# Top-k attention with a PReLU feed-forward: pairs prepared earlier, the last batch in another order, statistics from halves of fp32

## The chip, the cores and the metric

The kernel runs on one core of one Trainium2 chip. The metric is the device time of one execution in microseconds (us). Three runs of the kernel before gave 913.7 to 915.7, with a median of 914.88.

## What is computed

```python
def _attn_ref(q, k, v):                 # 8 batches, 8 heads, 576 tokens, 64 dims
    scores = (1 / sqrt(64)) * q @ k.T
    kth = np.partition(scores, -32)[..., -32]        # 32nd largest of each row
    scores = np.where(scores >= kth, scores, -1e9)
    attn = softmax(scores)
    return attn @ v

def reference(...):
    x = attn_out as (4608 tokens, 512)
    h = x @ w_in                        # 512 x 2048
    g = max(h, 0) + alpha * min(h, 0)
    return g @ w_out                    # 2048 x 512
```

## The kernel before, in words

**Tiles, pairs, batches.** The unit of the attention is a tile: 128 query rows against 576 keys. Two heads form a pair, whose queries and keys lie transposed in one buffer (`qkT`, one head in each half of the partitions). A pair has nine tiles (TPP = 9): tiles j = 0 to 7 are the four 128-row chunks of its two heads (chunk j // 2, head j % 2), and tile 8 holds the last 64 rows of both heads. There are 32 pairs (NPAIR), so NT = 288 tiles; four pairs form a batch of 576 tokens. P0 = 28 is the first pair of the last batch, N0 = 252 its first tile.

**What a tile needs.** TensorE computes the scores (L314). ScalarE shifts them by a guessed threshold of the row (L323), counts with a Sign pass how many lie above it (L329) and takes the exponential (L334). VectorE flips signs so that the wanted element is among the 24 largest (L345), finds them (L355, L370, L372), picks the limit and makes the mask (L419). GpSimd multiplies mask and exponential (L429); the last six tiles are multiplied on VectorE (L426). A DMA transposes the weights (L442), TensorE multiplies them with v (L488), and the result is divided by its row sum: `av_rz` on VectorE and `av_out` on ScalarE (L517).

**Preparing a pair.** The threshold comes from each row's mean and spread, which `prep_plan` (L166) works out for a pair in seventeen steps: q and k are transposed on TensorE (L175, L188, L196) and copied to `qkT` by ScalarE (L178, L192, L200); q is copied a second time, as bf16, to `qTb` (L180, L201); the 128 x 130 Gram matrix of k is built from fp32 operands (L206); `pe_r`, `dve_p` and `pe_s` (L212 to L241) turn it into the sums, for which `qTb` is read; eight small VectorE steps make the threshold. The transposes and the Gram matrix share one PSUM buffer (tag `pa`), and `pr`, `st` and the products with v (`pu`) share two (tag `pd`).

**The feed-forward.** Once a block of tokens is normalised and transposed (`x_turn`, L544), `mlp_steps` (L626) yields its steps: `ph` steps for the first product, each with a ScalarE activation (L644), and for each 128 tokens three `pz` steps with one copy to the output tile (L661). A block of 128 tokens has four `ph` and three `pz` steps.

**The order is written by hand.** The whole program is laid out tick by tick, one tile per tick (L758 to L842). In tick n the tile n + 1's scores are issued, flip works on tile n - 1, the search on tiles n - 2 and n - 3, and mask and weights on tile n - 7. `put(tick, engine, f)` places other work; a pair's steps stand at fixed distances before `BASE[p]` (L284), and its loads 18 ticks before it (L760). Feed-forward steps wait in the queue `back` and are taken from its front against a credit of 1.9 a tick at a cost of 0.9 or 1.5 (L787 to L799): one a tick, or two where `nb` is 2. Each engine executes its instructions strictly in this order.

**The last batch.** Its first two pairs run nine tiles each; the last two (PA, PB) alternate by chunk (L154). For these, `av_last`, `rz_last` and `out_last` (L521 to L542) handle one chunk of both pairs at a time, and each chunk is then a feed-forward block of 128 tokens.

Of the kernel before, what the change touches and what calls it, by code (L numbers as in the profile page):

```python
# [30 lines left out]
def kernel(  # L31
# [10 lines left out]
    nc = tc.nc  # L42
    B, H, S_, D = q.shape
# [5 lines left out]
    NPAIR = (B * H) // 2  # L49
    KPB = H // 2  # L50
    TPP = 9
    NT = NPAIR * TPP
# [4 lines left out]
    V1 = D + 1  # L57
    HC = S // 2
    P0 = NPAIR - KPB
    N0 = P0 * TPP  # L60
# [29 lines left out]
    prep = main.enter_context(tc.tile_pool(name="prep", bufs=2))  # L90
# [5 lines left out]
    ps_d = main.enter_context(tc.tile_pool(name="ps_d", bufs=2, space=PS))  # L96
# [30 lines left out]
    pairs = {}  # L127
# [21 lines left out]
                          vf[hA + 1, 64:S, :].rearrange("(c p) d -> p c d", p=128))  # L149

    ORDER = [divmod(n, TPP) for n in range(N0)]
    ORDER += [(p, j) for p in (P0, P0 + 1) for j in range(TPP)]
    PA, PB = P0 + 2, P0 + 3
    ORDER += [(p, j) for js in ((0, 1), (8,), (2, 3), (4, 5), (6, 7)) for p in (PA, PB) for j in js]  # L154
    units, unit_of = [], {}
    n = 0
    while n < NT:
        m = 1 if ORDER[n][1] == 8 and ORDER[n + 1][1] != 8 else 2
# [1 line left out]
            unit_of[n + i] = (n, m, i)  # L160
        units.append((n, m))
        n += m
    BASE = {p: TPP * p for p in range(P0)}
    BASE.update({P0: N0, P0 + 1: N0 + 8, PA: N0 + 14, PB: N0 + 20})

    def prep_plan(p):  # L166
        d = pairs[p]
        GK = GKs[p % 2]
        ns = slice(p * TPP, p * TPP + TPP)

        def pe_q():
            d["qkT"] = qkTs[p % NQ]
            d["pq"] = ps_a.tile([128, 512], FP32, name="pq", tag="pa")
            for c in range(4):
                nc.tensor.transpose(d["pq"][:, c * 128:(c + 1) * 128], d["q"][:, c, :], ident_f)  # L175

        def act_q():
            nc.scalar.copy(d["qkT"][:, 0, 0:512], d["pq"])  # L178
            d["qTb"] = prep.tile([128, S], BF16, name="qTb", bufs=2)
            nc.scalar.copy(d["qTb"][:, 0:512], d["pq"])  # L180

        def act_v():
            nc.scalar.copy(d["v"][:, :, 0:D], d["st_v"])
# [14 lines left out]

        def act_t():
            nc.scalar.copy(d["qkT"][:, :, 512:S], d["pt"])  # L200
            nc.scalar.copy(d["qTb"][:, 512:S], d["pt"][:, 0, :])  # L201

        def pe_g():
            d["pg"] = ps_a.tile([128, 130], FP32, name="pg", tag="pa")
            for c in range(5):
                nc.tensor.matmul(d["pg"], d["k"][:, c, 1:129], d["k"][:, c, :],  # L206
                                 start=(c == 0), stop=(c == 4))

        def act_g():
# [2 lines left out]
        def pe_r():  # L212
            d["P"] = prep.tile([128, S], BF16, name="P", bufs=1)
            d["pr"] = []
            for n0, n1 in ((0, 512), (512, S)):
                pr = ps_d.tile([128, n1 - n0], FP32, name="pr", tag="pd")
                for r in (slice(0, 64), slice(64, 128)):
                    nc.tensor.matmul(pr[r], GK[r, 1 + r.start:65 + r.start], d["qTb"][r, n0:n1],
                                     start=True, stop=True)
                d["pr"].append((n0, n1, pr))  # L220

        def dve_p():
            d["km"] = prep.tile([128, 2], BF16, name="km", bufs=2)
            nc.vector.tensor_tensor(d["km"], GK[:, 0:1].to_broadcast([128, 2]), bones, ALU.mult)
            for n0, n1, pr in d["pr"]:
                nc.vector.tensor_tensor(d["P"][:, n0:n1], pr, d["qTb"][:, n0:n1], ALU.mult)  # L226

        def pe_s():
            st = ps_d.tile([128, 2, TPP], FP32, name="st", tag="pd")
# [55 lines left out]
        dvx = "dve" if p < 2 else "dvx"  # L285
# [195 lines left out]
    def x_tiles(b):  # L481
        if b not in xb:
            xb[b] = prep.tile([128, 4, DM], BF16, name="xb", bufs=1)
            xm[b] = prep.tile([64, DM], BF16, name="xm", bufs=1)

    def av_one(o_, d, wT, side, cs):
        for c in range(5):
            nc.tensor.matmul(o_, wT[:, 4 * side + c, cs], d["v"][:, 5 * side + c, :],  # L488
                             start=(c == 0), stop=(c == 4))
# [12 lines left out]
    def av_rz(p, g):  # L502
        d = pairs[p]
        d["rz", g] = rz = attn.tile([128, 6], FP32, name="rz", bufs=4)
        nc.vector.reciprocal(rz[:, 0:4], d["pu", g][:, 0:4, D])
        if g == 1:
            nc.vector.reciprocal(rz[0:64, 4:6], d["pu", g][0:64, 4:6, D])
# [10 lines left out]

    pul = {}

    def av_last(i):  # L521
        m = 128 if i < 4 else 64
        pul[i] = pu = ps_d.tile([128, 4, V1], FP32, name="pu", tag="pd")
        for s, p in enumerate((PA, PB)):
            d = pairs[p]
            for side in range(2):
                cs = slice(0, 128) if i < 4 else slice(64 * side, 64 * side + 64)
                av_one(pu[0:m, 2 * s + side, :], d, d["wT", i] if i < 4 else d["wTm"], side, cs)

    def rz_last(i):  # L530
        m = 128 if i < 4 else 64
        rz = attn.tile([128, 6], FP32, name="rz", bufs=4)
        nc.vector.reciprocal(rz[0:m, 0:4], pul[i][0:m, :, D])
        pul[i] = pul[i], rz

    def out_last(i):
        m = 128 if i < 4 else 64
        pu, rz = pul.pop(i)
        dst = xb[B - 1][:, i, :] if i < 4 else xm[B - 1]
        nc.vector.tensor_tensor(  # L540
            dst[:, 256:512].rearrange("p (s d) -> p s d", s=4), pu[0:m, :, 0:D],
            rz[0:m, 0:4].unsqueeze(2).to_broadcast([m, 4, D]), ALU.mult)  # L542

    def x_turn(b, chunks):  # L544
        for i in chunks:
            c0 = (b * S + 128 * i) % NX
            if b == B - 1:
                c0 = b * S % NX + (64 + 128 * i if i < 4 else 0)
            if i < 4:
                nc.sync.dma_start_transpose(xT[:, :, c0:c0 + 128], xb[b][:, i, :])  # L550
            else:
                nc.sync.dma_start_transpose(xT[:, :, c0:c0 + 64], xm[b])
# [63 lines left out]
    banks = [0, 0]  # L616
# [66 lines left out]
    last = {4: (t7 - 64, 128)}  # L683
# [8 lines left out]
    with tc.manual_schedule(engines={E.PE, E.Activation, E.DVE, E.Pool, E.SP}):  # L692
        cal = {}

        def put(tick, eng, f):
            cal.setdefault((tick, eng), []).append(f)
# [15 lines left out]
        def tail_of(n, wn):  # L712
            wp, wj = ORDER[wn]
            b = wp // KPB
            if wp < PA:
                if wj == 3:
                    put(n + 3, "pe", lambda: av(wp, 0))
                    put(n + 4, "dve", lambda: av_rz(wp, 0))
                    put(n + 6, "act", lambda: av_out(wp, 0))
                    if wp % KPB == KPB - 1 and b >= 5:  # L720
                        put(n + 6, "end", lambda: x_turn(b, (0, 1)))
                        put(n + 8, "end", lambda: feed(b * S + 256))
                if wj == 8:
                    put(n + 4, "pe", lambda: av(wp, 1))
                    put(n + 5, "dve", lambda: av_rz(wp, 1))
                    put(n + 7, "act", lambda: av_out(wp, 1))
                    if wp % KPB == KPB - 1:
                        put(n + 7, "end", lambda: x_turn(b, range(2 if b >= 5 else 0, 5)))
                        put(n + 9, "end", lambda: feed((b + 1) * S))
            elif (wj == 8 or wj % 2) and wp == PB:  # L730
                i = wj // 2
                dt = 3 if n < NT else 2
                put(n + dt, "pe", lambda: av_last(i))
                put(n + dt + 1, "dve", lambda: rz_last(i))
                put(n + dt + 1, "dvx", lambda: out_last(i))
                put(n + dt + 1, "dvx", lambda: x_turn(b, (i,)))
                put(n + dt + 2, "end", lambda: back.extend(mlp_steps(*last.pop(i))))

        load(0, nc.scalar)
        load(1)  # L740
# [9 lines left out]
        back = deque((a, c, 1.0, 0) for a, c in weight_steps())  # L750
# [5 lines left out]
        n = 0  # L756
        end = max(NT + 24, 0)
        while n < end or back or after:  # L758
            for p in range(2, NPAIR):
                if n == max(0, BASE[p] - (18 if p < PB else 17)):  # L760
                    load(p)
                    plan(p)
                if n == max(0, BASE[p] - 13):
                    load_v(p)
            banks[0] = 2 if n >= NT else 1 if n >= BASE[NPAIR - 1] - 10 else 0
            if n + 1 < NT and unit_of[n + 1][2] == 0:
                scores(n + 1)
            while after:
# [1 line left out]
            if n < NT:  # L770
                n0, m, i = unit_of[n]
# [210 lines left out]
```

## Time and profile before

| | us |
|---|---|
| median of three runs | 914.88 |
| the profiled execution | 914.6 |
| its span, first to last instruction | 912.8 |
| VectorE busy | 843.2 |
| ScalarE busy | 810.9 |
| TensorE busy | 758.1 |
| GpSimd busy | 430.1 |
| VectorE's first flip (tile 0) | 19.68 |
| VectorE's last flip (tile 287) | 869.31 |

The span starts with the first instruction and ends with the last; the execution's own time is 1.8 us longer. PE is TensorE's matmul row and PEld its weight loads; DVE is VectorE, ACT ScalarE, POOL GpSimd, SP the queue that issues most DMAs. A row of the timeline begins with its start and its duration. L numbers are lines of the kernel before.

### The profile page before, as it was taken

The numbers are of one execution on the slowest core, as the hardware profiler recorded it, in microseconds if no ns is written. First come the engines' busy times: TensorE is split into PE (matmuls) and PEld (weight loads), VectorE is DVE, ScalarE is ACT, GpSimd is POOL, SyncE is SP. The second block draws the span as 40 slices with busy tenths as digits, with TensorE's granted clock in tenths as the row PEclk, the third lists the DMA queues.
The fourth block names the chain that finished last, engine by engine and source line by source line (L and its number), as shares of the span: only waits on it lengthen the run. The fifth ranks groups of instructions, "written<-read, shape, count | busy, mean of one in ns | idle before, by whom it ended". The sixth has DMA issues, their size and how long they took to land.

```text
span 912.8 us, 21132 instructions
## 1 busy us (share of the span) xinstructions
PE 758.1 (83%) x5907; PEld 464.1 (51%) x5907; DVE 843.2 (92%) x5301; ACT 810.9 (89%) x1894; POOL 430.1 (47%) x629
## 2 busy tenths in 40 slices
PE   5866788778968799878968889878988887899796
PEld 3544555445544456444544446545555545556564
DVE  3899989999999999999999999999999999789950
ACT  4999999899998999999998999999999997789732
POOL 0364545555455554555545555555555554345500
PEclk9666779799988999999988999999999998999699
DMA  6699645544556575554557656554566554354341
GB/s 152 118 167 200 138 80 105 111 89 89 133 104 116 85 120 122 108 102 99 130 100 112 105 103 116 111 116 94 115 118 120 115 122 98 68 98 76 75 94 39
DMA packets 343022, 99.54 MB, mean 109 GB/s; under 512 B 335200, under 2 KB 335216, under 8 KB 342896
## 3 DMA queue, kind: packets, MB, share of 16 engines
q1 hardware_dynamic: 340544, 95.71, 54.5%
q0 software_dynamic: 1152, 2.10, 1.7%
q8 instruction: 49, 0.80, 0.4%
q14 instruction: 77, 0.63, 0.2%
q10 hardware_dynamic: 1200, 0.30, 0.2%
HBM read 36.71 MB, written 9.44 MB: 51 GB/s over the span
## 4 chain that ended last, share of the span: by engine, by line
DVE 78%; PE 10%; ACT 7%; issue 2%; POOL 1%; DMA 1%; ACTq 0%; SPq 0%; DVEq 0%; POOLq 0%
DVE C L355 26%; DVE y L345 12%; DVE mk L419 12%; DVE C L372 10%; DVE L L370 9%; PE ph L638 3%; DVE P L226 2%; PE pz L656 2%; ACT b L323 2%; ACT h L329 1%; PE ps L314 1%; DVE L L389 1%; DVE KK L393 1%; DVE EQ L383 1%; ACT e L334 1%
## 5 line engine op out<-in xcount | busy, mean ns | idle before, releaser
L429 POOL TENSOR_TENSOR w<-mk,e 128x576 bf16<-128x576 bf16 x250 | 318.8, 1275 | 355.3 <-DVE mk L419 185.3
L355 DVE MAX8 C<-y 128x8 f32<-128x96 f32 x1728 | 418.7, 243 | 0.1
L314 PE MATMUL ps<-qkT 64*128 64x288 f32 (+1 forms) x1280 | 254.9, 478 | 23.2 <-ACT b L323 22.6
L323 ACT ACTIVATE b<-ps,NT 128x576 f32<-128x576 f32 x288 | 201.9, 758 | 4.7 <-PE ps L314 4.6
L329 ACT ACTIVATE h<-b 128x576 bf16<-128x576 f32 x288 | 203.0, 705 | 1.6
L638 PE MATMUL ph<-xT,w_in_b 128*128 128x128 bf16 (+2 forms) x1088 | 154.7, 290 | 44.0 <-ACT gT L644 35.2
L314 PEld LDWEIGHTS ps<-qkT 64*128 64x128 f32 (+1 forms) x1280 | 134.5, 196 | 82.6 <-ACT b L323 43.7
L334 ACT ACTIVATE e<-b 128x1152 bf16<-128x1152 f32 (+1 forms) x159 | 174.5, 1097 | 1.5 <-POOL w L429 1.3
L370 DVE MAX8 L<-C 128x8 f32<-128x48 f32 x864 | 162.5, 188 | 0.1
L345 DVE TENSOR_SCALAR y<-b,SG 128x576 int32<-128x576 int32 x288 | 147.1, 511 | 8.9 <-POOL SG L339 8.5
L419 DVE TENSOR_SCALAR mk<-b,KP 128x576 bf16<-128x576 f32 x282 | 143.5, 509 | 0.0
L638 PEld LDWEIGHTS <-w_in_b 128*128 128x128 bf16 x1088 | 86.0, 101 | 106.8 <-issue 82.0
L656 PE MATMUL pz<-w_out_b,gT 128*128 128x512 bf16 x576 | 138.6, 380 | 0.0
L644 ACT ACTIVATE gT<-ph 128x512 bf16<-128x512 f32 x144 | 87.9, 615 | 33.9 <-PE ph L638 33.9
L372 DVE MATCH_REPLACE8 C<-L,C 128x48 f32<-128x48 f32 x576 | 108.2, 188 | 0.0
L488 PE MATMUL pu<-v_bf,wT 128*128 128x65 bf16 (+1 forms) x1600 | 71.6, 202 | 21.0 <-DVE P L226 11.3
L656 PEld LDWEIGHTS <-gT 128*128 128x128 bf16 x576 | 53.2, 98 | 70.3 <-issue 13.7
L488 PEld LDWEIGHTS <-wT 128*128 128x128 bf16 (+1 forms) x1600 | 67.2, 106 | 33.4 <-issue 16.1
L339 POOL TENSOR_SCALAR SG<-S_all 128x1 int32<-128x1 f32 x288 | 64.9, 225 | 26.9 <-ACT h L329 26.9
L429 POOL TENSOR_TENSOR wm<-mk,e 128x576 bf16<-128x576 bf16 x32 | 40.8, 1274 | 51.7 <-DVE mk L419 50.4
L329 ACT ACTIVATION_READ_ACCUMULATOR h<-b 128x1 f32 x288 | 63.0, 219 | 0.0
L517 ACT ACTIVATE xb<-pu,rz 128x64 bf16<-128x64 f32 x240 | 57.6, 357 | 5.3 <-DVE C L355 3.0
(102 smaller groups left out, 804.9 us busy)
## 6 DMA issues: line engine op xcount, KB each, us to landing
out_dram<-o_sb SPq DMA_DIRECT2D x35, 256.0 KB, 2.4
st_q<-in_q_dram SPq DMA_DIRECT2D x64, 128.0 KB, 3.0
st_v<-in_v_dram SPq DMA_DIRECT2D x64, 128.0 KB, 2.7
kst<-in_k_dram SPq DMA_DIRECT2D x62, 128.0 KB, 2.8
w_stage<-in_moe_w_out_dram SPq DMA_DIRECT2D x16, 256.0 KB, 3.1
w_in_b<-in_moe_w_in_dram POOLq DMA_DIRECT2D x8, 256.0 KB, 6.7
wT<-w SPq DMA_TRANSPOSE x128, 3.3
st_q<-in_q_dram SPq DMA_DIRECT2D x32, 32.0 KB, 2.7
```

Source lines behind the costliest of these rows:

```text
L314: nc.tensor.matmul(o_, l_, r_, start=True, stop=True)
L323: nc.scalar.activation(t["b"].rearrange("p (a c) -> p a c", a=2), t["ps"], AF.Identity, bias=NT0[:, p * TPP + j:p * TPP + j + 1], scale=ON ...
L329: nc.scalar.activation(h, tiles[n]["b"], AF.Sign, accum_out=S_all[:, n:n + 1])
L334: nc.scalar.activation(e, tiles[n0]["bu"], AF.Exp, scale=scl)
L345: nc.vector.tensor_scalar(t["y"].bitcast(I32), t["b"].bitcast(I32), FLIP, SG[:, n:n + 1], ALU.bitwise_xor, ALU.bitwise_xor)
L355: return [lambda g=g: nc.vector.max(out=C[:, n % TPP, g, :], in_=t["y"][:, g * SEG:(g + 1) * SEG]) for g in range(NSEG)]
L370: ops.append(lambda r=r, src=src: nc.vector.max(out=L[:, 8 * r:8 * r + 8], in_=src))
L372: ops.append(lambda r=r, src=src: nc.vector.match_replace(out=C2, in_to_replace=L[:, 8 * r:8 * r + 8], in_values=src, imm_value=NEG))
L419: nc.vector.tensor_scalar(t["mk"], t["b"], row_limit(n), None, ALU.is_ge)
L429: nc.gpsimd.tensor_tensor(dst, t["mk"], t["e"], ALU.mult)
L638: nc.tensor.matmul(hold[f][:, i, :], w_in_b[:, kk, (f + i) * 128:(f + i + 1) * 128], xT[:, kk, c0:c0 + tb], start=(kk == 0), stop=(kk == N ...
L656: nc.tensor.matmul(pz[0:m], hold["gT"][:, f, r0:r0 + m], w_out_b[:, f, :], start=False, stop=(f == NFT - 1))
```

## The change

1. **Statistics.** The bf16 copy of q (`qTb`) is gone. A helper views an fp32 buffer as bf16 and takes each element's upper half, so `pe_r` and `pe_s` read q from `qkT`, and the Gram matrix takes bf16 operands out of the fp32 keys. `dve_p` multiplies with fp32 q.
2. **Earlier preparation.** `BASE[p]` becomes nine ticks smaller for each pair after pair 11, and nine smaller again after pair 20; pairs 11 and 20 themselves move by four ticks.
3. **Last batch.** All four pairs go by chunk. `av_last` and its two companions run for two pairs at a time (g = 0 or 1), and all of the batch takes this way. The two-step rate of the queue begins at tick N0 + 2 rather than N0 + 10.

```diff
-    ORDER += [(p, j) for p in (P0, P0 + 1) for j in range(TPP)]
-    PA, PB = P0 + 2, P0 + 3
-    ORDER += [(p, j) for js in ((0, 1), (8,), (2, 3), (4, 5), (6, 7)) for p in (PA, PB) for j in js]
+    LAST = range(P0, NPAIR)
+    ORDER += [(p, j) for p in LAST[:3] for j in (0, 1)] + [(p, 8) for p in LAST[:2]]
+    ORDER += [(P0, 2), (P0, 3), (P0 + 3, 0), (P0 + 3, 1)] + [(p, 8) for p in LAST[2:]]
+    ORDER += [(p, j) for p in LAST[1:] for j in (2, 3)]
+    ORDER += [(p, 2 * i + h) for i in (2, 3) for p in LAST for h in range(2)]
...
-    BASE = {p: TPP * p for p in range(P0)}
-    BASE.update({P0: N0, P0 + 1: N0 + 8, PA: N0 + 14, PB: N0 + 20})
+    LEAD1, LEAD2 = 11, 20
+    BASE = {p: TPP * (p - (p > LEAD1) - (p > LEAD2)) for p in range(NPAIR)}
+    BASE[LEAD1] -= 4
+    BASE[LEAD2] -= 4
...
+        def high(x):
+            return x.bitcast(BF16).rearrange("p (n h) -> p n h", h=2)[:, :, 1]
...
-            d["qTb"] = prep.tile([128, S], BF16, name="qTb", bufs=2)
-            nc.scalar.copy(d["qTb"][:, 0:512], d["pq"])
...
-            nc.scalar.copy(d["qTb"][:, 512:S], d["pt"][:, 0, :])
...
-                nc.tensor.matmul(d["pg"], d["k"][:, c, 1:129], d["k"][:, c, :],
+                nc.tensor.matmul(d["pg"], high(d["k"][:, c, 1:129]), high(d["k"][:, c, :]),
...
+            d["qTb"] = high(d["qkT"][:, 0, :])
...
-                nc.vector.tensor_tensor(d["P"][:, n0:n1], pr, d["qTb"][:, n0:n1], ALU.mult)
+                nc.vector.tensor_tensor(d["P"][:, n0:n1], pr, d["qkT"][:, 0, n0:n1], ALU.mult)
...
-    def av_last(i):
+    def av_last(i, g):
+        x_tiles(B - 1)
         m = 128 if i < 4 else 64
-        for s, p in enumerate((PA, PB)):
-            d = pairs[p]
+        for s in range(2):
+            d = pairs[P0 + 2 * g + s]
...
-            if wp < PA:
+            if wp < P0:
...
-            elif (wj == 8 or wj % 2) and wp == PB:
-                i = wj // 2
+            elif (wj == 8 or wj % 2) and wp % 2:
+                i, g = wj // 2, (wp - P0) // 2
                 dt = 3 if n < NT else 2
-                put(n + dt, "pe", lambda: av_last(i))
-                put(n + dt + 1, "dve", lambda: rz_last(i))
-                put(n + dt + 1, "dvx", lambda: out_last(i))
-                put(n + dt + 1, "dvx", lambda: x_turn(b, (i,)))
-                put(n + dt + 2, "end", lambda: back.extend(mlp_steps(*last.pop(i))))
+                put(n + dt, "pe", lambda: av_last(i, g))
+                put(n + dt + 1, "dve", lambda: rz_last(i, g))
+                put(n + dt + 1, "dvx", lambda: out_last(i, g))
+                if g == 1:
+                    put(n + dt + 1, "dvx", lambda: x_turn(b, (i,)))
+                    put(n + dt + 2, "end", lambda: back.extend(mlp_steps(*last.pop(i))))
...
-                if n == max(0, BASE[p] - (18 if p < PB else 17)):
+                if n == max(0, BASE[p] - 18):
...
-            banks[0] = 2 if n >= NT else 1 if n >= BASE[NPAIR - 1] - 10 else 0
+            banks[0] = 2 if n >= NT else 1 if n >= N0 + 2 else 0
...
-            nb = 1 if n < BASE[NPAIR - 1] - 10 else 2
+            nb = 1 if n < N0 + 2 else 2
```

More of the change, by code (lines that the diff above doesn't have):

```diff
@@ L519 @@
     pul = {}
-    def av_last(i):
+    def av_last(i, g):
+        x_tiles(B - 1)
         m = 128 if i < 4 else 64
-        pul[i] = pu = ps_d.tile([128, 4, V1], FP32, name="pu", tag="pd")
-        for s, p in enumerate((PA, PB)):
-            d = pairs[p]
+        pul[i, g] = pu = ps_d.tile([128, 4, V1], FP32, name="pu", tag="pd")
+        for s in range(2):
+            d = pairs[P0 + 2 * g + s]
             for side in range(2):
@@ L528, in av_last, with rz_last, out_last @@
                 av_one(pu[0:m, 2 * s + side, :], d, d["wT", i] if i < 4 else d["wTm"], side, cs)
-    def rz_last(i):
+    def rz_last(i, g):
         m = 128 if i < 4 else 64
         rz = attn.tile([128, 6], FP32, name="rz", bufs=4)
-        nc.vector.reciprocal(rz[0:m, 0:4], pul[i][0:m, :, D])
-        pul[i] = pul[i], rz
-    def out_last(i):
+        nc.vector.reciprocal(rz[0:m, 0:4], pul[i, g][0:m, :, D])
+        pul[i, g] = pul[i, g], rz
+    def out_last(i, g):
         m = 128 if i < 4 else 64
-        pu, rz = pul.pop(i)
+        pu, rz = pul.pop((i, g))
         dst = xb[B - 1][:, i, :] if i < 4 else xm[B - 1]
         nc.vector.tensor_tensor(
-            dst[:, 256:512].rearrange("p (s d) -> p s d", s=4), pu[0:m, :, 0:D],
+            dst[:, 256 * g:256 * g + 256].rearrange("p (s d) -> p s d", s=4), pu[0:m, :, 0:D],
             rz[0:m, 0:4].unsqueeze(2).to_broadcast([m, 4, D]), ALU.mult)
```

## The prediction, made before the run

> **What bounds the kernel now.** I read the page's busy times and chain first, then the windows, to see where VectorE (DVE) is not full.
>
> ```profile
> span 912.8 us, 21132 instructions
> PE 758.1 (83%) x5907; PEld 464.1 (51%) x5907; DVE 843.2 (92%) x5301; ACT 810.9 (89%) x1894; POOL 430.1 (47%) x629
> ...
> DVE 78%; PE 10%; ACT 7%; issue 2%; POOL 1%; DMA 1%; ACTq 0%; SPq 0%; DVEq 0%; POOLq 0%
> ...
> 20.00:140.00 120.00, 88.98 (x565) 57.72 (x565) 111.09 (x687) 116.93 (x263) 56.85 (x86) 0.69 0.75 139
> ...
> 300.00:400.00 100.00, 88.69 (x723) 52.63 (x724) 99.90 (x633) 95.61 (x232) 52.34 (x74) 0.98 0.61 112
> ...
> 740.00:860.00 120.00, 103.73 (x822) 65.20 (x821) 107.98 (x675) 101.88 (x236) 56.39 (x81) 0.91 0.47 92
> ...
> 880.00:890.00 10.00, 10.00 (x125) 7.30 (x123) 0.71 (x5) 2.97 (x5) 0.00 (x0) 1.00 0.44 94
> ...
> 900.00:913.00 13.00, 6.65 (x62) 4.03 (x59) 0.00 (x0) 2.71 (x5) 0.00 (x0) 0.88 0.13 47
> ```
>
> The columns after the length are PE, weight loads, DVE, ACT and POOL. From 300 to 400 DVE is busy 99.90 of 100 us: there nothing counts but DVE's own instructions. Four places differ: the start, where DVE has nothing yet; 20 to 140, where DVE loses 8.9 us and ACT is busy 116.93 of 120; 740 to 860, where DVE loses 12.0; and from 880 on, where DVE is done and PE works off feed-forward blocks. The change must earn its time in these, or lose it.
>
> **The start: -2.6 us.**
>
> ```profile
> 6.67 0.59 ACT L180 CAST qTb<-pq 128x512 bf16<-128x512 f32 x1
> ...
> 9.78 0.22 ACT L201 CAST qTb<-pt 128x64 bf16<-128x64 f32 x1
> 10.05 2.53 PE L206 MATMUL pg<-kst 128*128 128x130 f32 x10 [0.47 <-ACT qTb L201]
> ...
> 12.96 0.69 PE L218 MATMUL pr<-qTb,GK 64*64 64x512 bf16 x4 [0.37 <-ACT GK L210]
> ...
> 19.68 0.52 DVE L345 TENSOR_SCALAR y<-b,SG 128x576 int32<-128x576 int32 x1 [2.81 <-POOL SG L339]
> ```
>
> Pair 0's preparation is one chain up to the first flip at 19.68. Both casts of q stand on it, since the next transposes wait for their PSUM buffer: about 0.5 and 0.15 us go. The Gram step takes 2.53 us as ten fp32 records and becomes five bf16 matmuls. No row shows them: half of 2.53 (1.27) is the upper bound, five at the 0.04 us each of warm products with v (20 in 0.80, row 883.99 below) the lower, 0.2; I take 0.6, near the four bf16 matmuls of L218 (0.69, with a colder clock and wider). That saves 1.9. Reading halves at a four-byte step is shown by no row either: nothing as one end, twice the 0.69 at L218 as the other; I take nothing, as the fp32 words it steps over are read at the same addresses now. Sum -0.5 - 0.15 - 1.9 = -2.6, bounds -1.2 to -3.
>
> **From 20 to 140: -3 us.**
>
> ```profile
> L180 ACT CAST qTb<-pq 128x512 bf16<-128x512 f32 x32 | 19.7, 616 | 0.0
> ...
> L201 ACT CAST qTb<-pt 128x64 bf16<-128x64 f32 x32 | 8.2, 256 | 0.0
> L226 DVE TENSOR_TENSOR P<-pr,qTb 128x512 bf16<-128x512 f32 x32 | 21.9, 683 | 5.5 <-PE pr L218 5.5
> ...
> L426 DVE SCALAR_TENSOR_TENSOR w<-b,KP,e 128x576 bf16<-128x576 f32 x6 | 4.5, 807 | 0.0
> ```
>
> A pair loses 616 + 256 = 872 ns of ACT. Some five pairs (1 to 5) are prepared here, 4.4 us, where ACT is the fullest engine; DVE idles 8.9. The gain lies between 0 (if the DMAs, busy 0.75 here, set the pace) and 6; I take 3. From 140 to 740 the 0.87 us per pair on ACT, and the Gram time on PE, are hidden behind a full DVE: nothing. DVE's product P keeps its 683 ns: one input grows from bf16 to fp32, so no gain; the dearest fused row, 807 ns for 576 elements, would make 717 of it, +1.1 us over 32 pairs. I take 0.
>
> **The two leads: +1.5 us.** Pairs 11 and 20 are prepared four ticks off the usual grid, so that three preparations fall into some 13 ticks. By the tick loop, `pe_r` of pair 11 (85) then falls on the tick of pair 8's first product with v, and pair 20 likewise: in the built order `pu` directly follows `pr`. Both take the two `pd` buffers, so PE waits until DVE has read `pr`, with the next scores queued behind it. Before, that order stands only at pairs 30 and 31.
>
> ```profile
> 768.04 1.26 PE L488 MATMUL pu<-v_bf,wT 128*128 128x65 bf16 x20 [3.00 <-DVE P L226]
> ...
> PE pu L488 <- DVE P L226: 7.5, 4, 2.9
> ```
>
> At 768 PE waited 3.00 us and DVE then 1.2 (in the 4.2 of `rz` below). The second row, for 200 to 740, has four such waits with 7.5 us in all, while DVE stayed full. So a lead costs 0 to 3; the queue of feed-forward steps is empty in ticks 79 to 87 and 151 to 159, which leaves PE slack. I take 0.75 each.
>
> **Ticks 252 to 287: -2.8 us.** DVE's waits from 740 to 880, and flips of tiles 252, 262 and 287:
>
> ```profile
> DVE rz L505 <- PE pu L488: 4.2, 5, 1.2
> DVE y L345 <- POOL SG L339: 2.8, 3, 1.3
> DVE sq L251 <- ACT MM L247: 2.5, 2, 1.7
> DVE P L226 <- PE pr L218: 2.4, 1, 2.4
> ...
> 755.99 0.52 DVE L345 TENSOR_SCALAR y<-b,SG 128x576 int32<-128x576 int32 x1
> ...
> 794.48 0.51 DVE L345 TENSOR_SCALAR y<-b,SG 128x576 int32<-128x576 int32 x1
> ...
> 869.31 0.50 DVE L345 TENSOR_SCALAR y<-b,SG 128x576 int32<-128x576 int32 x1
> ...
> L540 DVE TENSOR_TENSOR xb<-pu,rz 128x256 bf16<-128x256 f32 x4 | 1.7, 419 | 0.0
> ...
> L533 DVE RECIPROCAL rz<-pu 128x4 f32<-128x4 f32 x4 | 0.7, 172 | 4.8 <-PE pu L488 4.8
> ```
>
> Now three preparations (29, 30, 31) lie in ticks 246 to 270, together with the feed-forward of batch 6: ticks 252 to 262 take 38.5 us, 3.85 each, against 2.99 for the 25 after. In the new order the last preparation ends near tick 259, so the 4.9 us of waits for `sq` and `P` go. The 7.0 for `rz` and `y` come from PE and ACT running late under feed-forward steps. Those were queued in ticks 262 to 278; now chunks 0, 4 and 1 of the last batch come at 276, 278 and 284 and keep two steps a tick running until 290. By the credit that is 1.9 us of PE a tick beside scores and products with v: close to a whole tick. Longer exposure raises the 7.0, relief from three preparations lowers it; I take 5.5, with bounds 2 and 15. DVE gains work: five more `out_last` at 419 ns, 2.1 us, while ten `rz` replace eleven (no change). It also gets a wait: `out_last` for chunk 0 writes the single `xb` buffer in tick 266, one tick after batch 6's last transposes out of it are issued; before, ACT first wrote it in 268. A transpose lands some 2.6 us after issue (row 858.71 below), two queue; DVE could wait 0 to 4, with masks and search behind it: 1.5. Sum: 5.5 + 1.5 + 2.1 - 11.9 = -2.8, bounds -8 to +8.
>
> **The tail: -9.7 us.**
>
> ```profile
> 858.71 1.29 SPq L550 DMA_TRANSPOSE xT<-xb  x1
> ...
> 861.33 5.76 PE L638 MATMUL ph<-xT,w_in_b 128*128 128x128 bf16 x64 [3.16 <-DMA xT<-xb]
> ...
> 874.92 0.16 DVE L533 RECIPROCAL rz<-pu 128x4 f32<-128x4 f32 x1
> ...
> 875.57 1.20 SPq L550 DMA_TRANSPOSE xT<-xb  x1
> ...
> 883.99 0.80 PE L488 MATMUL pu<-v_bf,wT 128*128 128x65 bf16 x20
> ...
> 898.58 3.75 PE L638 MATMUL ph<-xT,w_in_b 128*128 128x128 bf16 x64
> 902.17 1.03 PE L652 MATMUL pz<-w_id_b,xT 128*128 128x512 bf16 x4
> 903.03 3.62 PE L656 MATMUL pz<-w_out_b,gT 128*128 128x512 bf16 x16
> ```
>
> Now all five chunks of the last batch run from 861.33 to 903.03 + 3.62 = 906.65, a full one in 906.65 - 898.58 = 8.07; the span ends 6.15 later. In the new order only chunks 2 and 3 are left when the tiles end. Chunk 2 is complete with tile 279, as chunk 1 was, so its transpose takes the place of the one at 875.57 (all times here relative to the last flip). It lands 861.33 - 858.71 = 2.6 later, 878.2. Chunk 2's first six steps come before the last products with v (ticks 292 to 294 of the queue): 3.6 for `ph` and 14 of 20 `pz` matmuls, 3.1, to 884.9. The products (0.7) end at 885.6, DVE's division and the issue (874.92 to 875.57) at 886.2, the transpose at 888.9, chunk 3 at 896.9: 9.7 earlier. Bounds: -12 if chunk 2 starts sooner, 0 if chunk 1 is late by as much. The output DMA and the flag's check stay.
>
> **Sum.** -2.6 - 3.0 + 1.5 - 2.8 - 9.7 = -16.6: span 896.2, plus the 1.8 around it 898.0. The profiled run (914.6) is 0.3 below the median of the three, which I leave out.
>
> **Rivals.**
>
> *Better hidden* (0.17): relieved of casts and preparations, ACT and PE keep up with two steps a tick. Waits 2, leads 0, 6 won early: -2.6 - 6 - 6.3 - 9.7 = -24.6, 890.0. For it speaks the full DVE in 300 to 400 with ACT at 95.61; against it 740 to 860.
>
> *The tail's clock* (0.10). PE now waits twice for a transpose, with little else to do.
>
> ```profile
> 852.00:860.00 8.00, 5.01 (x44) 3.77 (x42) 7.95 (x48) 6.51 (x13) 3.96 (x7) 0.50 0.43 84
> ...
> 889.00:891.60 2.60, 1.14 (x20) 1.02 (x19) 0.15 (x1) 0.65 (x2) 0.00 (x0) 1.00 0.00 0
> ```
>
> The granted clock was 0.50 in the broken-up work of 852 to 860, and the `ph` group after it took 5.76 instead of 3.75; a wait of about 1.5 us near 890 left it at 1.00. Two chunks begun at 0.50 cost 2 x 2.0: 902.0. [...]
>
> *The tail doesn't shorten* (0.08): chunk 1 is still unfinished when the tiles end, chunks 2 and 3 queue behind it, and the 9.7 is lost: 907.7.
>
> *Slower* (0.05): feed-forward under the tiles makes PE and ACT the bound, and the 3.85 us a tick of ticks 252 to 262 also holds for the 25 after: 96.3 instead of 869.31 - 794.48 = 74.8, +21.4, with the rest -13.8: 922.2. It decides from 74.8 + 13.8 + 1.8 = 90.4, 3.6 us a tick. Against it: preparations fell into the 3.85, and they are gone.
>
> **Numbers.** The forecast has 0.60, within 892 to 906. I give 889 to 908, which takes in the tail rivals and the edge of the better one. A measurement here tells about 0.2% (1.8 us) from no change. Faster: 0.94; same 0.01; slower 0.05.
>
> **What would show it.** The first flip near 17.1; DVE idle in 20 to 140 near 6; PE waits of 2 to 3 us behind `pr` near ticks 85 and 157; tick 252 to 287 shorter, without waits of `sq` or `P`; an `out_last` that waits for a transpose of `xb`; two chunks of feed-forward after the last flip, and a tail of 34 us from it rather than 43.5. The forecast is wrong if flips come over 3.2 us apart after tile 276, if the leads show up as gaps in DVE's row, or if `P` takes longer than 0.7 us.

## The result, and the profile after

The changed kernel takes 907.41 us (median of four runs, 906.11 to 911.0) beside 915.24 for the kernel before (913.7 to 915.7): a ratio of 0.9909, with an interval of 0.9882 to 0.9937. That is 7.8 us faster, where 17 were forecast from the medians: 907.4 lies outside the 892 to 906 that the forecast itself covers, and just inside the wider 889 to 908. Run once more beside the last experiments it had 907.19 and a ratio of 0.9912 (0.9888 to 0.9937).

The profiled execution of the changed kernel took 906.11 us, the shortest of the four, so its span lost 8.6 us rather than 7.8. First the head of its page, and its windows in the order of those of before (PE, weight loads, DVE, ACT, POOL, granted clock, DMA share, GB/s):

```profile
span 904.2 us, 20676 instructions
...
PE 737.7 (82%) x5747; PEld 433.0 (48%) x5747; DVE 845.1 (93%) x5305; ACT 787.6 (87%) x1809; POOL 430.8 (48%) x629
```

```profile
20.00:140.00 120.00, 87.06 (x547) 51.86 (x547) 112.03 (x698) 114.59 (x253) 58.39 (x87) 0.69 0.76 143
300.00:400.00 100.00, 86.07 (x675) 48.18 (x674) 99.82 (x628) 93.19 (x219) 51.18 (x74) 0.95 0.55 109
740.00:860.00 120.00, 111.07 (x984) 70.67 (x983) 115.65 (x715) 106.79 (x233) 60.79 (x88) 0.97 0.45 86
880.00:890.00 10.00, 7.68 (x71) 5.12 (x69) 0.85 (x5) 2.01 (x4) 0.00 (x0) 0.90 0.14 40
```

ACT lost 23 us of work and PE 20, and neither is what the span lost (8.6): DVE has 1.9 more. It still loses 8.0 us in 20 to 140 (8.9 before), and only 4.4 in 740 to 860 (12.0 before).

Reading the start of each tile's flip as a clock lays the 8.6 us out along the kernel. The windows between flips then say whether a stretch changed by DVE's work or by its waiting; the three stretches that moved most are ticks 84 to 107, 155 to 166 and 252 to 287, first of the kernel before, then of the changed one:

```profile
270.07:336.50 66.43, 54.45 (x384) 30.54 (x385) 66.43 (x418) 62.44 (x152) 34.51 (x49) 0.95 0.63 104
475.62:507.09 31.47, 22.90 (x164) 13.49 (x165) 31.47 (x202) 28.71 (x67) 16.38 (x23) 0.89 0.70 114
755.99:869.31 113.32, 96.00 (x807) 63.81 (x805) 101.30 (x631) 92.32 (x213) 52.75 (x75) 0.88 0.44 82
```

```profile
267.03:338.54 71.51, 56.20 (x409) 31.17 (x409) 68.26 (x430) 61.36 (x146) 34.55 (x49) 0.90 0.54 98
478.54:514.00 35.46, 24.42 (x200) 14.41 (x199) 33.02 (x212) 27.15 (x64) 16.41 (x23) 0.85 0.53 101
763.45:867.23 103.78, 97.61 (x929) 64.41 (x928) 99.43 (x613) 89.32 (x188) 52.85 (x75) 0.97 0.46 88
```

| stretch | forecast | change | DVE work | DVE waits |
|---|---|---|---|---|
| start, to the first flip | -2.6 | -2.3 | | |
| ticks 0 to 36 (to some 130 us) | -3.0 | -0.9 | -0.1 | -0.9 |
| ticks 84 to 107 (lead of pair 11) | +0.75 | +5.1 | +1.8 | +3.3 |
| ticks 155 to 166 (lead of pair 20) | +0.75 | +4.0 | +1.6 | +2.4 |
| ticks 252 to 287 | -2.8 | -9.5 | -1.9 | -7.7 |
| from the last flip to the end of the span | -9.7 | -6.5 | | |
| the three other stretches | 0 | +1.7 | +0.5 | +1.2 |
| sum | -16.6 | -8.6 | | |

DVE's 66.43 of 66.43 us and 31.47 of 31.47 say that before, neither lead's stretch had any wait. Now DVE has ten to twelve instructions more in each, 1.8 + 1.6 = 3.4 us: preparation done earlier, which comes off later. It costs nothing over the whole kernel, and the prediction didn't count it on either side. The 3.3 + 2.4 = 5.7 us of waiting do cost. The end, without the moved 3.4, won 6.2.

**The start** went as sketched. PE and DVE of the changed kernel:

```profile
9.53 0.70 PE L210 MATMUL pg<-kst 128*128 128x130 bf16 x5 [0.35 <-ACT qkT L205]
10.60 0.69 PE L223 MATMUL pr<-qkT,GK 64*64 64x512 bf16 x4 [0.37 <-ACT GK L214]
...
17.34 0.52 DVE L350 TENSOR_SCALAR y<-b,SG 128x576 int32<-128x576 int32 x1 [2.81 <-POOL SG L344]
```

The Gram step takes 0.70 us (2.53 before; 0.6 was assumed), at a granted clock of 1.00 both times. The `pr` step reads every second bf16 of fp32 words and takes the same 0.69, also at 1.00. DVE's product kept its price too, 683 ns before and 684 now:

```profile
L231 DVE TENSOR_TENSOR P<-pr,qkT 128x512 bf16<-128x512 f32 x32 | 21.9, 684 | 6.3 <-PE pr L223 6.1
```

**The first lead.** DVE and PE around 270 us, and the row of PE's waits from 140 to 740, which had 7.5 us in four waits before:

```profile
269.74 0.81 DVE L231 TENSOR_TENSOR P<-pr,qkT 128x512 bf16<-128x512 f32 x2
270.47 1.26 PE L493 MATMUL pu<-v_bf,wT 128*128 128x65 bf16 x20 [6.51 <-DVE P L231]
271.77 0.18 DVE L510 RECIPROCAL rz<-pu 128x4 f32<-128x4 f32 x1 [1.22 <-PE pu L493]
```

```profile
PE pu L493 <- DVE P L231: 16.9, 8, 6.5
```

PE stood still for 6.51 us, not for the two or three expected. The place is the one the prediction names (`pu` behind `pr`, both in the two `pd` buffers), but DVE reads `pr` only in its work of the next tick. PE's whole lead over DVE is spent there, and DVE waits for PE (1.22 us at `rz`) and twice more in the ticks after, 3.3 us in all.

**Ticks 252 to 287.** The waits for `sq` and `P` are gone, as forecast; so are those for `rz` and `y`, against the forecast. DVE's waits from 765 to 870:

```profile
DVE xb L546 <- DMA xT<-xb: 3.4, 1, 3.4
DVE y L350 <- POOL SG L344: 0.5, 2, 0.3
```

The one that is left is new: `out_last` waits 3.4 us for the transposes out of the single `xb` buffer (1.5 assumed).

**The tail.** PE and SP's queue of the changed kernel:

```profile
870.48 0.49 PE L493 MATMUL pu<-v_bf,wT 128*128 128x65 bf16 x10 [0.21 <-DMA wT<-w]
872.57 0.49 PE L493 MATMUL pu<-v_bf,wT 128*128 128x65 bf16 x10 [1.59 <-DMA wT<-w]
...
876.00 6.61 PE L644 MATMUL ph<-xT,w_in_b 128*128 128x128 bf16 x64 [2.94 <-DMA xT<-xb]
...
885.47 0.80 PE L493 MATMUL pu<-v_bf,wT 128*128 128x65 bf16 x20
...
890.03 3.75 PE L644 MATMUL ph<-xT,w_in_b 128*128 128x128 bf16 x64 [2.35 <-DMA xT<-xb]
...
894.48 3.62 PE L662 MATMUL pz<-w_out_b,gT 128*128 128x512 bf16 x16
```

Chunk 2 starts 8.8 us after the last flip, where 8.9 was forecast, and only two chunks are left. But its `ph` takes 6.61 us instead of 3.75, and all behind it is that much later. The windows say why (the clock is third from the end):

```profile
870.00:876.00 6.00, 1.25 (x23) 0.75 (x21) 5.72 (x29) 0.59 (x1) 0.00 (x0) 0.93 0.41 83
876.00:884.00 8.00, 8.00 (x72) 7.17 (x73) 1.83 (x12) 2.39 (x4) 0.00 (x0) 0.62 0.55 98
```

In the six us ahead PE worked for 1.25; in the eight after it had 0.62 of its clock.

### The profile page after: what moved, and what is told of

It reads as the page before. It is cut to its first block, busy times and chain, and to the rows that moved or that the text cites. A ratio compares the mean times of both kernels' runs of the same rounds, so it can differ in the third digit from the quotient of the medians.

```text
span 904.2 us, 20676 instructions
## 1 busy us (share of the span) xinstructions
PE 737.7 (82%) x5747; PEld 433.0 (48%) x5747; DVE 845.1 (93%) x5305; ACT 787.6 (87%) x1809; POOL 430.8 (48%) x629
## 5 line engine op out<-in xcount | busy, mean ns | idle before, releaser
L319 PE MATMUL ps<-qkT 64*128 64x288 f32 (+1 forms) x1280 | 258.8, 478 | 34.8 <-ACT b L328 34.8
L644 PE MATMUL ph<-xT,w_in_b 128*128 128x128 bf16 (+2 forms) x1088 | 161.8, 299 | 44.7 <-ACT gT L650 34.1
L644 PEld LDWEIGHTS <-w_in_b 128*128 128x128 bf16 x1088 | 87.9, 103 | 112.4 <-issue 81.5
L522 ACT ACTIVATE xb<-pu,rz 128x64 bf16<-128x64 f32 x224 | 53.9, 358 | 3.4 <-DVE C L360 2.5
```

The source lines that it names most:

```text
L319: nc.tensor.matmul(o_, l_, r_, start=True, stop=True)
L644: nc.tensor.matmul(hold[f][:, i, :], w_in_b[:, kk, (f + i) * 128:(f + i + 1) * 128], xT[:, kk, c0:c0 + tb], start=(kk == 0), stop=(kk == N ...
```

## The experiments

Theories after the result. **Collision**: what the leads cost is the product with v that meets `pr` of the prepared pair; move the product and the stall goes. **Clock**: the missing 3 us of the tail are chunk 2's `ph` at the fallen clock; keep PE busy ahead of it and they come back. Against both stood *crowding*: three preparations in some 13 ticks, and the feed-forward of the last batch, make PE and ACT the bound by their sheer amount, wherever a step stands. For the statistics, *only the start* stood against *start and the full ACT of 20 to 140*. In the experiments "the changed kernel" is the one above; each ratio is against the kernel before on the same chip. Spans, tails and windows are those of one profiled execution each, which need not be the median one (898.05 us for the four corrections together, 907.93 for chunk 3 sooner). One correction is worth 1 to 5 us, and of the single ones only that of both products has an interval clear of the changed kernel's 0.9882 to 0.9937; the readings of the others rest on the rows, not on the totals.

### The product with v two ticks later (collision, with a control in it)

```diff
+                    l = 2 if wp + 3 in (LEAD1, LEAD2) else 0
-                    put(n + 3, "pe", lambda: av(wp, 0))
+                    put(n + 3 + l, "pe", lambda: av(wp, 0))
```

(and the same `l` for `av_rz` and `av_out`.)

> The changed kernel, with the first product with v of pairs 8 and 17 (and the two steps behind it) two ticks later, so that it no longer falls on the tick in which the early pairs 11 and 20 take both PSUM buffers. Theory: the flips of tiles 84 to 107 and 156 to 170 fell behind by 4.9 and 4.0 us, of which 1.6 each is VectorE work that only moved and the rest, 3.3 and 2.4, comes from TensorE standing 6.5 us behind VectorE's product P; without the collision the two stretches lose about 2 us each, 4 to 5 us less in all, and the run takes 4 to 5 us less. Rival: three preparations in 13 ticks are too many for ScalarE and TensorE whatever the order; then VectorE still idles 2 to 3 us at each lead and the time stays within 1 us of the changed kernel.

Measured: 905.22 us, 0.9894 (0.9866 to 0.9923), span 902.8. Ticks 84 to 107 fell from 71.51 to 68.50; ticks 155 to 166 stayed at 35.40 (35.46). The edit moves the products of pairs 8 and 17, and it is pair 16's product that meets pair 20's preparation, since pair 11's lead has by then moved all of the grid by nine ticks. So the second lead was left as it was, and serves as a control: the stall went only where the colliding product was moved, and with it only a part of the 4 to 5 us expected.

### Both colliding products later

```diff
+                    l = 2 if 9 * wp + 13 in (BASE[LEAD1] - 10, BASE[LEAD2] - 10) else 0
```

> As e1_av_later, but with the product that really meets the second lead: after the first shift it is pair 16's, not pair 17's, that falls on pair 20's tick; so the first products of pairs 8 and 16 come two ticks later. Theory of the collision: in e1 the first lead lost 2.1 us instead of 5.1 (1.6 of it moved work), and the second, left as it was, 4.0; now the second loses 1.6 to 2.2 as well, and the last flip stands about 5 us before that of the changed kernel, apart from what the first 130 us vary. Rival: the second lead meets feed-forward and preparation work that the first doesn't, and still loses 3.5 to 4.

Measured: 902.11 us (901.11 to 902.96), 0.9854 (0.9838 to 0.9870), span 900.3. Windows between the flips of the same ticks 84 to 107 and 155 to 166, and DVE's waits from 140 to 740, all of them:

```profile
270.07:338.27 68.20, 54.78 (x403) 29.32 (x402) 67.94 (x430) 61.64 (x146) 34.53 (x49) 0.92 0.54 102
477.40:510.23 32.83, 26.28 (x197) 14.27 (x195) 32.83 (x212) 27.05 (x66) 16.38 (x23) 0.79 0.58 109
```

```profile
DVE P L231 <- PE pr L223: 1.3, 1, 1.3
DVE rz L510 <- PE pu L493: 0.3, 1, 0.3
```

DVE has the same 430 and 212 instructions as in the changed kernel, and is full (67.94 of 68.20, 32.83 of 32.83). Collision holds; crowding falls, because all three preparations still stand in these ticks. Of the two leads' +9.1 us, (71.51 - 68.20) + (35.46 - 32.83) = 5.9 were the stall, and the rest is moved work (3.4 by the instructions' busy time).

### The first `out_last` two ticks later

```diff
-                put(n + dt + 1, "dvx", lambda: out_last(i, g))
+                put(n + dt + (3 if (i, g) == (0, 0) else 1), "dvx", lambda: out_last(i, g))
```

> The changed kernel, with the first division of the last batch (chunk 0, first two pairs) two ticks later, so that the transposes out of the single xb buffer have landed. Theory: VectorE's wait of 3.4 us for them goes; as VectorE is full in the ticks around it, the last flip comes about 3 us earlier and the run takes about 3 us less. Rival: TensorE is the bound in these ticks under two feed-forward steps a tick, and the 3.4 us come back as waits for scores or products before the last flip; then the time changes by under 1 us.

Measured: 903.93 us (900.45 to 908.97), 0.9878 (0.9834 to 0.9923), span 901.1. Ticks 265 to 267 went from 9.19 to 5.38, so the wait of 3.4 was on the path where it stood; the ticks around it gave 1.7 back (a wait of 1.1 for `rz` among them), and ticks 252 to 287 are 2.1 shorter in all (101.69), not the 3 expected.

### PE kept busy ahead of chunk 2 (clock)

```diff
                 put(n + dt, "pe", lambda: av_last(i, g))
+                if (i, g) == (3, 0):
+                    put(n + dt, "pe", keep_busy)
...
+    def keep_busy():
+        kb = ps_m.tile([128, DM], FP32, name="kb", tag="misc")
+        for f in range(12):
+            nc.tensor.matmul(kb, w_out_b[:, f, 0:128], w_out_b[:, f, :], start=True, stop=True)
```

It adds twelve matmuls that nobody reads.

> The changed kernel with twelve more matmuls of 512 columns on TensorE, whose result nobody reads, right before the first feed-forward steps of chunk 2, where TensorE waited 2.94 us for a transpose. Theory: chunk 2's 64 matmuls took 6.61 us instead of 3.75 because the granted clock had fallen in the waits; kept busy, they take 3.75 to 4, and the tail from the last flip becomes about 34 us instead of 37.0: 2.5 to 3 us less. Rival: they are slow for another reason (the activations between them, the weight loads), and take 6.6 again; the time is the same or up to 1 us longer.

Measured: 905.68 us (902.84 to 906.89), 0.9892 (0.9875 to 0.9910), span 901.0. PE in the tail:

```profile
872.67 2.75 PE L539 MATMUL kb<-w_out_b 128*128 128x512 bf16 x12
...
875.64 3.76 PE L649 MATMUL ph<-xT,w_in_b 128*128 128x128 bf16 x64 [0.22 <-DMA xT<-xb]
```

The idle work fills the wait for the transpose (0.22 left), `ph` takes 3.76, and the tail is 34.1 us instead of 37.0: the forecast's 34. Clock holds, and nearly all that was missing in the tail is back.

### Chunk 3's last product a tick sooner

```diff
+                e = 1 if (i, g) == (3, 1) else 0
-                put(n + dt, "pe", lambda: av_last(i, g))
+                put(n + dt - e, "pe", lambda: av_last(i, g))
```

(and `- e` on its `rz_last`, `out_last`, `x_turn` and feed-forward.)

> The changed kernel with the last products with v (and division, transpose and feed-forward steps of chunk 3) one tick sooner, between chunk 2's ph and pz steps. Theory: chunk 3's transpose then lands while TensorE works on chunk 2's pz steps (4.5 us), so that the wait of 2.35 us before chunk 3 goes: a tail of 34 to 35 us instead of 37.0. Rival: the transposes of the last weights land later than chunk 2's ph steps end, TensorE waits for them instead, and the tail stays within 1 us.

Measured: 906.38 us, 0.9893 (0.9874 to 0.9913), span 906.1; tail 35.75, 1.2 shorter, where 2 to 3 were expected. (The span is longer for ticks far from the edit: it doesn't touch them.) PE on chunk 3:

```profile
890.04 1.95 PE L644 MATMUL ph<-xT,w_in_b 128*128 128x128 bf16 x32
891.92 0.19 PE L482 MATMUL ptot<-ones_f,tot 128*1 128x1 f32 x2
893.60 1.95 PE L644 MATMUL ph<-xT,w_in_b 128*128 128x128 bf16 x32 [1.49 <-ACT gT L650]
```

The wait of 2.35 for chunk 3's transpose is gone, and a part of it comes back: the check of the flag (`ptot`), which stood in that wait, now stands between two halves of `ph`, and the second waits 1.49.

### The statistics undone, and the statistics alone

The first run is the changed kernel with `qTb` copied and fp32 Gram operands again; the second is the kernel before with part 1 of the change only.

```diff
+            d["qTb"] = prep.tile([128, S], BF16, name="qTb", bufs=2)
+            nc.scalar.copy(d["qTb"][:, 0:512], d["pq"])
...
-                nc.tensor.matmul(d["pg"], high(d["k"][:, c, 1:129]), high(d["k"][:, c, :]),
+                nc.tensor.matmul(d["pg"], d["k"][:, c, 1:129], d["k"][:, c, :],
```

> The changed kernel with the statistics as before (bf16 copy of q, Gram matrix from fp32), so only the earlier preparation and the new last batch. Theory: the statistics are worth the 2.3 us at the first flip and about 1 us up to tile 35, and in the last batch the relief of ScalarE and TensorE; the first flip is again at 19.7, the leads cost 1 to 3 us more than in the changed kernel, and the run takes 4 to 8 us more than the changed kernel. Rival: behind a full VectorE the statistics gain nothing but the start, and the run takes 2 to 3 us more.

> The kernel before with only the new statistics (halves of fp32, no bf16 copy of q). Theory: it wins the 2.3 us at the first flip, 0 to 3 in the stretch up to tile 34, nothing from 140 to 740, and 1 to 4 in ticks 252 to 287, where three preparations ran beside the feed-forward: 3 to 6 us less than before. Rival: its only gain is the start, 2 to 3 us.

Measured: undone 909.91 us, 0.9931 (0.9907 to 0.9954), first flip at 19.59; alone 913.2 (911.36 to 918.38), 0.9979 (0.9962 to 0.9996), first flip at 17.17. Part 1 is worth about 2 us both ways by the ratios (2.7 and 2.5 by the medians), as both rivals had it and less than either theory; the first flips, 2.5 and 2.3 earlier, account for it. The profile of the statistics alone has one gain later on, in ticks 252 to 287 (113.32 us before):

```profile
755.03:865.87 110.84, 91.76 (x786) 60.21 (x785) 101.31 (x632) 91.08 (x209) 52.79 (x75) 0.88 0.41 84
```

DVE's work is the same there, and its waits are 2.5 us shorter, 1.8 of that at `sq` and `P`, steps of the preparation; in this execution 1.4 more up to tile 36 and 0.5 more in the tail hide it. In the changed kernel, whose preparations lie elsewhere, these ticks took 103.78 and 103.20 us, and 104.25 with the old statistics. In the stretch for which the gain was forecast, the 0.87 us of ACT per pair bought nothing that can be seen. Tile 36 (near 130 us) was flipped at 130.45 us before, at 129.36 with the statistics alone, and at 127.16 in the changed kernel; over all profiles of this study it stands at 130.4 on average in the three with old statistics and at 128.4 in the eleven with new ones (126.4 to 130.4): again the start, and a scatter of 2 us either way.

### The weights' preparation spread thinner

What does set the pace in 20 to 140? In the changed kernel PE waits up to 5.3 us there for a transpose of weights, while SP's queue also issues the transposes of `w_in` (2.91 us for the one at 74.80) and the DMA engines are 0.98 busy (60 to 100 us). Here the loads and transposes of `w_in` are spread over 32 ticks.

```diff
-                                 w_in(f // 2) if f < 8 and f % 2 == 0 else None)),
+                                 w_in(f // 4) if f % 4 == 0 else None)),
...
-            yield (lambda: None), (lambda f=f: w_in2(f // 2) if f < 8 and f % 2 == 1 else None)
+            yield (lambda: None), (lambda f=f: w_in2(f // 4) if f % 4 == 3 else None)
```

> The changed kernel with the loads of w_in and the transposes of it spread over 32 ticks instead of 16. Theory: the 2.3 us won at the first flip are lost again by tile 36 (127.2 to 130.4 us in six profiles with the new statistics, 130.45 before), because near 80 us TensorE waits 5 to 6 us for a transpose of the weights on full DMA engines; thinned, that wait falls under 2 us and tile 36 comes at 125 to 127. Rival: ScalarE, which also converts the weights in these ticks, sets the pace; tile 36 stays at 128 to 130.

Measured: 904.49 us (902.39 to 905.67), 0.9878 (0.9850 to 0.9905); the changed kernel beside it 907.19, with intervals that overlap. The wait near 80 us fell from 4.5 us to 2.5, but with the waits at other places PE waited longer for `wT` in 20 to 140, 9.9 us in three waits beside 7.3 in two in the changed kernel, and tile 36 came at 127.17 beside 127.36. The edit moved the waits and didn't take them away, so it doesn't tell whether they set the pace: inconclusive. TensorE's clock is another candidate. Between tile 0 and tile 36 it was granted at 0.66 in both kernels, but a lower one didn't go with a longer stretch. The changed kernel run again, and the kernel with the first product later:

```profile
17.37:127.36 109.99, 80.76 (x441) 48.22 (x438) 101.91 (x630) 105.09 (x229) 52.50 (x79) 0.60 0.83 152
17.31:129.82 112.51, 76.80 (x439) 45.05 (x437) 101.97 (x630) 105.22 (x229) 52.56 (x79) 0.67 0.78 149
```

That speaks against the clock as the cause of the scatter, and leaves open whether it sets the pace.

### The earlier preparation alone

The kernel before with part 2 only:

```diff
-    BASE = {p: TPP * p for p in range(P0)}
-    BASE.update({P0: N0, P0 + 1: N0 + 8, PA: N0 + 14, PB: N0 + 20})
+    LEAD1, LEAD2 = 11, 20
+    BASE = {p: TPP * (p - (p > LEAD1) - (p > LEAD2)) for p in range(NPAIR)}
+    BASE[LEAD1] -= 4
+    BASE[LEAD2] -= 4
```

> The kernel before with only the earlier preparation (BASE, the two leads), with its old statistics and its old last batch. Theory: tiles 252 to 287 gain most of what the changed kernel gained there, since the waits came from three preparations beside feed-forward steps (104 to 106 us instead of 113.3, of which 3.2 is work that only moved), the leads take 5.7 us of that back, and the tail stays at 43.5: 0 to 3 us faster than before. Rival: the new order of the last batch was what shortened these ticks; then they take over 108 and the kernel is 1 to 4 us slower than before.

Measured: 911.0 us (909.72 to 912.85), 0.9948 (0.9931 to 0.9966), 4.3 us less than the kernel before beside it (0 to 3 expected), span 910.7; tail 43.54, as before. Ticks 252 to 287 and DVE's waits there:

```profile
767.88:867.16 99.28, 86.39 (x706) 55.65 (x704) 97.95 (x609) 86.29 (x197) 52.63 (x75) 0.90 0.42 85
```

```profile
DVE y L347 <- POOL SG L341: 0.9, 2, 0.7
DVE rz L507 <- PE pu L490: 0.2, 1, 0.2
```

This settles whose gain the stretch is: 99.28 instead of 113.32, with DVE 97.95 us busy. The preparations in ticks 246 to 270 had caused nearly all of its 12 us of waits, those for `rz` and `y` too: 1.3 are left. The new order of the last batch takes 4.5 back (103.78, or 104.25 with the old statistics: the wait of 3.4 at `xb`, and five more `out_last`) and earns 6.5 in the tail.

### The corrections together

Four of them (both products later, first `out_last` later, PE kept busy, chunk 3 sooner); then these with the weights' preparation spread and with the flag's check five ticks later (`put(n + 11, "end", final_flag)` for `n + 6`); beside the last, the changed kernel once more.

> The changed kernel with all four edits: products of pairs 8 and 16 two ticks later, first division of the last batch two ticks later, twelve idle matmuls before chunk 2, last products one tick sooner. If the four causes are separate, their gains add: 5 (leads) + 2 (xb) + 3 (clock) + 2 to 2.5 (last product) = about 12 us less than the changed kernel, near 895 us and a span near 892. Rival: with the clock up, chunk 2's ph steps end before the last weights' transposes land, and one of the two tail edits gives nothing: near 898.

> The kernel with the four edits together, with the weights' DMAs spread out as in e10 and the flag's check five ticks later, so that it no longer stands between chunk 3's ph steps (a wait of 1.5 us there). Theory: 1.5 us from the flag and 2 to 3 from the start, 3 to 4.5 us less than the four edits (895.9): near 892. Rival: the spread weights delay the first feed-forward and give the start's gain back; near 895.

> The changed kernel once more, beside these. Its first four executions gave 906.1 to 911.0. Theory: it lies within 904 to 911 again, and its profile shows the same lead losses (5 and 4 us) and chunk 2 at a fallen clock. Rival: the first profile was a lucky or unlucky one, and these places look different.

Measured: four 895.88 us (893.92 to 898.92), 0.9785 (0.9762 to 0.9809), span 896.1, tail 33.87; six 895.02 (893.50 to 895.71), 0.9775 (0.9754 to 0.9797), span 892.4, tail 33.24. Both beat both kernels; the last two corrections together give 0.9 us, which is within the spread and nearer to the rival's 895 than to the 892 expected. The six on PE:

```profile
864.89 2.75 PE L539 MATMUL kb<-w_out_b 128*128 128x512 bf16 x12
867.95 3.76 PE L649 MATMUL ph<-xT,w_in_b 128*128 128x128 bf16 x64 [0.31 <-DMA xT<-xb]
...
877.18 3.75 PE L649 MATMUL ph<-xT,w_in_b 128*128 128x128 bf16 x64
881.62 3.62 PE L667 MATMUL pz<-w_out_b,gT 128*128 128x512 bf16 x16
```

Neither `ph` shows a fallen clock (3.76 and 3.75 us), chunk 3's runs in one piece, and of the waits for a transpose of `xb` only 0.31 us is left. In the tail of the changed kernel, run again, the lost clock lay elsewhere:

```profile
875.39 5.06 PE L644 MATMUL ph<-xT,w_in_b 128*128 128x128 bf16 x64 [2.92 <-DMA xT<-xb]
...
887.89 5.36 PE L644 MATMUL ph<-xT,w_in_b 128*128 128x128 bf16 x64 [2.36 <-DMA xT<-xb]
```

Both chunks lose some, 1.3 and 1.6 us over 3.75 (the clock was 0.73 from 876 to 880 and 0.66 from 888 to 893), where the first profile had one losing 2.9; the tail is the same (37.08). The leads are too (71.67 and 35.73 us beside 71.51 and 35.46).

## Why the prediction was right and wrong

The direction was right, and four of its five places were the right ones; the sum was 8.0 us too good, about half of its 16.6. Against its terms, that is start 0.3, ticks 0 to 36 2.0, leads 4.2, tail 3.2 and drift elsewhere 1.7, less 3.4 by which the end did better.

- **Start (-2.6): right**, -2.3. The assumptions on bf16 halves (0.6 us for the Gram step, 0.70 measured; nothing for the step of four bytes, 0.69 before and after) held, and `P` at 0 held (683 and 684 ns). The colder clock that the estimate names for L218 is not in the trace: it was 1.00 there.
- **20 to 140 (-3): failed.** The step was that ACT, the fullest engine, sets the pace, so that its 4.4 us come back in part. The lower end of that step's own range was the truth: no gain that stands out of a scatter of 2 us. That ACT was relieved is in its row (116.93 to 114.59), and DVE's idle time went from 8.9 to 8.0 only, where near 6 was the sign. What sets the pace instead is open: the one edit made for it only moved the DMA waits, and the stretch's length doesn't follow the clock (0.69 in this window in both kernels), which no run changed on purpose.
- **Two leads (+1.5): the mechanism right, the size wrong**, 5.7 us of waits. The failing step was sizing PE's wait by the row of before (3.00 us) and taking a full DVE as proof that it stays hidden. Before, such waits ended within PE's lead over DVE (2.9 us at most from 140 to 740, where DVE had no wait); 6.51 us did not. The two runs that move the product show it, one with the other lead as control. The gaps in DVE's row at the leads, the prediction's own sign of being wrong, came; its other two didn't (flips 2.81 us apart after tile 276, `P` at 0.68 us).
- **Ticks 252 to 287 (-2.8): too cautious**, -6.2 without the moved work. The step that failed is the 5.5 us put on two steps a tick: it took the waits for `rz` and `y` as feed-forward's doing, and the run with earlier preparation alone shows them as the preparations', all but 1.1. The wait at `xb` was found, at 3.4 instead of 1.5. (The upper bound of this place adds up to +9.2 from its terms, not to +8.)
- **Tail (-9.7): the order right, the clock wrong**, -6.5. The difference is the rival *the tail's clock*, which got 0.10: one of its two losses (2.9 us, more than the 2.0 it put on a chunk) came in the first profile, both in the second (1.3 and 1.6), and PE kept busy brings them back. The reason given against it, a wait of 1.5 us that left the clock at 1.00, is no measure of two in a row, 1.59 and 2.94 with 0.49 us of work between them, after which the clock was 0.62. In the kernel before, it was down (0.51) from 848.5 on, after 3.5 us in which PE worked for 1.81, and no wait of PE in the ten us ahead was longer than 1.92 us.

```profile
845.00:848.50 3.50, 1.81 (x8) 0.92 (x8) 3.50 (x24) 3.47 (x7) 2.36 (x3) 1.00 0.29 54
848.50:852.00 3.50, 3.27 (x16) 2.24 (x17) 3.50 (x25) 3.50 (x13) 2.23 (x5) 0.51 0.50 95
```

- **The other rivals.** *Better hidden* came true for the end alone. *The tail doesn't shorten* fell, although its 907.7 is nearly the time that was measured: that is chance, as the tail did shorten by 6.5, and most of the rest was lost at the leads and before tile 36. *Slower* fell too: ticks 252 to 287 took 103.78 us, where *slower* needs 38.5 + 96.3 = 134.8.

One omission belongs to no term: the preparation moved out of the last ticks costs DVE its 3.4 us in the leads. The forecast left it out at both ends, so the sum didn't suffer, but the lengths of the leads and of ticks 252 to 287 have to be read without it.

## What to carry to other kernels

When a step is moved on a hand-written grid, look at which other steps then share its tick and its buffers. Here a producer that had to wait for a buffer until the consumer's next tick lost its whole lead at once (6.51 us), and two ticks of distance gave it back (2.4 us at most then). Ask of each wait on the bound engine whose work caused it by undoing one part: here the same row of waits had two candidate causes, and the wrong one was priced. At the end of a kernel like this one, where TensorE waits for transposes between short pieces of work, count the following block at the fallen clock (5.06 to 6.61 us instead of 3.75 here), or fill the wait (3.76).

## What the runs showed of the hardware

- **After two waits with little work between them the clock fell, at the same cost in two executions.** The waits were 1.59 and 2.94 us; 1.25 us of work in six were followed by 0.62 of the clock and 2.9 us of loss in one `ph` (6.61 beside 3.75). In the second execution, after waits of 1.81 and 2.92, both chunks lost (5.06 and 5.36, at clocks of 0.73 and 0.66; 2.9 together). Its second chunk came after a wait of 2.36 us; in the first execution one of 2.35 was followed by 1.00 and 3.75 us. 2.75 us of matmuls that nobody reads took the loss away (3.76). In the kernel before, the clock fell from 1.00 to 0.51 after 3.5 us in which TensorE worked for 1.81. No wait in these tails was longer than 2.94 us, and what decides when the clock falls was not shown.
- **bf16 halves of fp32 words cost TensorE no more here than packed bf16.** Five such Gram matmuls take 0.70 us where ten fp32 records took 2.53, and four `pr` matmuls 0.69 us with either source, all at a clock of 1.00. On VectorE, multiplying by fp32 instead of bf16 made no difference (684 and 683 ns for 512 elements out of PSUM).
